# Attention and feed-forward kernel: the product with the values shares three pairs of PSUM banks with the scores and is issued in six pieces

## The chip, the cores and the metric

The kernel runs on one core of a Trainium2 chip. Its engines are PE (TensorE: weight loads and matmuls into PSUM), DVE (VectorE), ACT (ScalarE), POOL (GpSimd) and SP (SyncE, which issues the DMAs). PSUM has eight banks, each of 128 partitions by 512 fp32 numbers. The metric is the device time of one execution in microseconds (us), median of several runs; lower is better.

## What is computed

```
scores = 0.125 * q @ k.T                        # batch 8, heads 8, sequence 576, head width 64
thresh = max(scores, row) - tau
p      = exp(scores - max) where scores >= thresh, else 0
x      = (p / (sum(p, row) + 1e-9)) @ v         # then heads side by side: x is (8, 576, 512)

x_prev = x shifted by one position, zeros first
xk, xr = x_prev + mu_k * (x - x_prev), x_prev + mu_r * (x - x_prev)
out    = sigmoid(xr @ w_r) * (relu(xk @ w_k)**2 @ w_v)     # w_k 512x1024, w_v 1024x512, w_r 512x512
```

## The kernel before

Work comes in 36 **jobs**. A job is one batch and one pair of heads (two of 64 wide, 128 partitions); the first batch's four pairs are each cut in two half jobs, so jobs 1 to 4 hold half the queries and 5 to 8 the other half. A full job has four units `P` of 128 queries for two heads, and one unit `T` for the last 64 queries of both: nine score tiles of 128 x 576. Per tile PE makes the scores (L559, for `T` L526, in the first job L543) as two halves of 288 columns in a pair of PSUM banks, tag `s`; DVE takes the row maximum (L605), ACT the exponential (L621), DVE the mask and the row sum (L629), POOL scales (L654), and DVE transposes in blocks of 32 (L671, for `T` L675). The scores keep the precision of fp32 with q and k each as a high and a low part, which DMAs bring together (`st`, from `hiq`, `loq`, `hik`, `lok`).

When all units of a job are transposed, `attend` multiplies by the values (L705): 144 matmuls of 32 x 64 array tiles, each of which the trace shows as two, so 288 pairs of a weight load and a matmul, into four banks of tag `w`. ACT copies the result to `xT` (L719) and `xE` (L726).

The feed-forward part takes 256 positions of a batch at a time, 18 chunks in all. A chunk has 96 matmuls with `w_k` (L843), 24 with `w_r` (L885) and 48 with `w_v` (L907); each weight and each operand is split in two parts, so a product takes three matmuls. Its PSUM tiles are also of tag `w`. The weights are brought and split in the first part of the run (20 pieces, L355 to L414).

The order on every engine is written by `Plan`. Each step (`add`) has an engine, an assumed time, operands and a key; `order` lists the steps greedily by the earliest start in its own arithmetic, then by the key, to which `NUDGE` adds a number for each kind of step. A buffer is handed out in turn, or to whoever comes first for the tags in `loose`. What the plan lists for an engine is then that engine's instruction order: an engine does not pass a waiting instruction. Two pairs of banks of `s` and four single banks of `w` fill PSUM.

```
ss = {y: psum("s", [P, 2, 512], 2) for y in ys}          # scores
os = [psum("w", [P, 512], 4) for _ in range(4)]          # product with the values
h  = psum("w", [P, 2, CH], 4)                            # feed-forward
KC, MV, RES = 2, 0.031, 3                                # KC: pieces of the product
```

Of the kernel before, what the change touches and what calls it, by code (L numbers as in the profile page):

```python
# [9 lines left out]
AF = mybir.ActivationFunctionType  # L10
# [30 lines left out]
class Step:  # L41
    __slots__ = (
        "eng", "occ", "lat", "fn", "key", "deps", "succ", "allocs", "idx", "missing", "ready",
        "start", "end", "kb", "soft", "att", "kind",
    )


class Plan:

    HOP, LATE, FROM, AHEAD = 0.05, 0.2, 200.0, 1000.0
    SOFT = {"DVE": 0.15, "ACT": 0.15}
    NUDGE = {
# [7 lines left out]
    }  # L62

    def __init__(self):
# [10 lines left out]

    def add(self, eng, occ, fn, reads=(), writes=(), key=0.0, lat=None, kb=0, wait=0.0, kind=None):
        s = Step()
        s.soft = self.SOFT.get(eng, 0.0) if self.soft else 0.0
        s.att = eng == "PE" and key < -500
        if s.att:  # L80
            key += 1000 - self.AHEAD
        s.eng, s.occ, s.fn, s.kb, s.kind = eng, occ, fn, kb, kind
        s.key = key + self.NUDGE.get(kind, 0.0)
# [36 lines left out]
        s.deps.discard(s.idx)  # L120
        self.steps.append(s)
        return s

    def order(self, loose=()):
# [15 lines left out]
        free = {}  # L140
# [4 lines left out]
        for s in steps:  # L145
            if s.missing == 0:
                open_[s.eng].add(s.idx)
        pipe = 0.0
        out = []
        placed = set()  # L150
# [21 lines left out]
        while len(out) < total:  # L172
            best = None
            for e, cand in open_.items():
                f = free[e]
                pick = None
                for i in cand:
                    s = steps[i]
                    t = when(s)
                    if t is None:  # L180
                        continue
                    t = max(t, f)
                    k = (t + s.soft, s.key, i, t)
# [7 lines left out]
            s = steps[i]  # L191
            open_[e].discard(i)
            s.start = t
            free[e] = t + s.occ
            if e == "DMA":
                pipe = max(pipe, t) + s.kb / 260.0
                s.end = max(t + 3.5, pipe + 2.5)
            else:
                s.end = t + s.lat
            for b in s.allocs:  # L200
# [10 lines left out]
            for j in s.succ:  # L211
# [3 lines left out]
                late = self.LATE if n.att and t > self.FROM else 0.0  # L215
                n.ready = max(n.ready, t + s.occ if same else s.end + self.HOP + late)
                if n.missing == 0:
# [12 lines left out]
def tile_threshold_attention_then_rwkv_ffn(  # L230
# [265 lines left out]
    def scores(unit, ss, key):  # L496
# [5 lines left out]
        if unit["kind"] == "T" and not job["plain"]:  # L502
# [17 lines left out]
            for h in range(2):  # L520
                for v_ in range(2):
# [11 lines left out]

                    add("PE", 0.264, mm, reads=[bd, r], writes=[ss[1]], key=key - 1000, lat=0.44, kind="pe1")
            return
        if job["plain"]:
# [13 lines left out]

            add("PE", 3.0, both, reads=[raw], writes=list(ss.values()), key=key - 1000, lat=3.25, kind="pe2")
            return
        for y in range(2):
            st1, st2 = job["st"][y]
            for j, l in enumerate((st1, st2)):
# [10 lines left out]

                add("PE", 0.264, mm, reads=[l, st1], writes=[ss[y]], key=key + 0.5 * y - 1000, lat=0.44, kind="pe3")

    def softmax(unit):
# [6 lines left out]
        sq, c = job["sq"], unit["c"]  # L576
        p = {y: (sq, (c, y)) for y in ys}

# [4 lines left out]

        ss = {y: psum("s", [P, 2, 512], 2) for y in ys}
        scores(unit, ss, float(n))
        for y in ys:
# [95 lines left out]
    def attend(job, key):  # L682
# [9 lines left out]
        tail = [(xE, (b % NE, hp))] if job["tail"] else []  # L692
        os = [psum("w", [P, 512], 4) for _ in range(4)]
        last = job["units"][-1]
        for o in os:
            add("PE", 0.0, lambda: None, reads=[(last["sm"], (RES, 1))], writes=[o, *main, *tail], key=-400.0, lat=0.0, kind="pe4")
        for k in range(KC):

            def mm(k=k):
                for j in range(k * NB // KC, (k + 1) * NB // KC):  # L700
                    for h in range(2):
                        hs = slice(h * D, (h + 1) * D)
                        for a in range(4):
# [8 lines left out]

            occ = (MV * n + 0.3) / KC
            add("PE", occ, mm, reads=[vt, sq], writes=os, key=key - 1000, lat=occ + 0.25, kind="pe5")
        for a in range(4):

            def put(a=a):
                to = x.get()[:, hp, 1 : 1 + SM].rearrange("p (c a i) -> p c a i", a=4, i=Q)
                A.activation(  # L719
                    to[:, cs[0] : cs[-1] + 1, a],  # L720
                    os[a].get()[:, 0 : mid - lo].rearrange("p (c i) -> p c i", i=Q),
                    AF.Copy,
                )

            def put_tail(a=a):
                A.activation(  # L726
                    xE.get()[:, hp, b % NE, 1 + a * QT : 1 + (a + 1) * QT], os[a].get()[:, mid - lo : n], AF.Copy
                )

            add("ACT", 0.16 if len(cs) == 4 else 0.11, put, reads=[os[a]], writes=main, key=key - 5, kind="act8")  # L730
            if job["tail"]:
                add("ACT", 0.07, put_tail, reads=[os[a]], writes=tail, key=key - 5, kind="act9")

# [14 lines left out]
    def ffn_chunk(kind, b0, g, key):  # L748
# [82 lines left out]
        for j in range(NFT // 2):  # L831
            h = psum("w", [P, 2, CH], 4)
            for f in range(2):
                y, o = divmod((2 * j + f) * P, 512)
                fs = slice(o, o + P)
                for ct in range(NCT):
# [10 lines left out]
                    c2 = ct - ct % 2  # L847
                    add("PE", 0.3585, mm, reads=[w, *([xk] if ct == 0 else [(xk, (0, c2)), (xk, (1, c2))])], writes=[h, *([(k2, (0, j))] if f == 0 and ct == 0 else [])], key=key, lat=0.53, kind="pe6")
            js = slice(2 * j, 2 * j + 2)
# [25 lines left out]
        for j in range(CH // P):  # L875
            ts = slice(j * P, (j + 1) * P)
            z = psum("w", [P, DM], 4)
            for ct in range(NCT):
# [8 lines left out]
                c2 = ct - ct % 2  # L887
                add("PE", 0.69, mm, reads=[w, *([xr] if ct == 0 else [(xr, (0, c2)), (xr, (1, c2))])], writes=[z, *([(sg, j)] if ct == 0 else [])], key=key, lat=0.86, kind="pe7")
            add("ACT", 0.49, lambda j=j, z=z: A.activation(sg.get()[:, j], z.get(), AF.Copy), reads=[z], writes=[(sg, j)], key=key - 20, kind="act14")
# [7 lines left out]
        for j in range(CH // P):  # L897
            ts = slice(j * P, (j + 1) * P)
            vps = psum("w", [P, DM], 4)
            for ft in range(NFT):  # L900
# [7 lines left out]

                add("PE", 0.69, mm, reads=[w, *([k2] if ft == 0 else [(k2, (0, ft // 2)), (k2, (1, ft // 2))])], writes=[vps], key=key, lat=0.86, kind="pe8")
            add(  # L910
# [65 lines left out]

    plan.order(loose=("w", "r"))
    plan.issue()
# [41 lines left out]
```

## Time and profile before

| | |
|---|---|
| median of 3 runs | 1134.08 us (1131.31 to 1139.18) |
| the profiled execution | 1133.43 us, of which the span from first to last instruction is 1131.3 us |
| PE busy | 922.5 us, 82% |
| DVE busy | 841.9 us, 74% |
| ACT, POOL busy | 649.1 us, 57%; 573.1 us, 51% |
| mean granted clock of PE | 0.921 of full speed |
| first product, last product | 25.2 us, 993.5 to 1000 us |

The busy time of an engine is the time in which any of its instructions runs by the profile; a matmul's end is modelled, so neighbours overlap. The share of one engine says little here, since the run has stretches of different kinds: the start, in which weights are prepared and the feed-forward work has not begun (to about 113 us), the stretch in which it begins (to about 353 us, the end of the 13th product), a steady stretch of 23 jobs, and after the last product a stretch of feed-forward work alone.

### The profile page before, as it was taken

Reading aid. Unit: us, or ns where it says so; the run is one execution under the profiler, and the core shown is the slowest. Engines: PE = TensorE matmul, PEld = TensorE weight load, DVE = VectorE, ACT = ScalarE, POOL = GpSimd, SP = SyncE. Lnnn points to the kernel's source line nnn. Section 1 sums busy time; section 2 is a strip of 40 time slices with the busy share of each in tenths; the row PEclk is TensorE's granted clock in tenths of the full one; section 3 lists DMA queues with packets and bytes.
Section 4 is the critical chain, followed back from the end, with each engine's and each line's share of the span. In section 5 each row is a group of like instructions: output and inputs, shape, how many; then the busy total and the mean of one; then the engine's idle time right before and its main releaser. Section 6 shows DMA issues by size and latency. Waiting matters only on the chain.

```text
span 1131.3 us, 35156 instructions
## 1 busy us (share of the span) xinstructions
PE 922.5 (82%) x14672; PEld 822.8 (73%) x14672; DVE 841.9 (74%) x1657; ACT 649.1 (57%) x1492; POOL 573.1 (51%) x582
## 2 busy tenths in 40 slices
PE   2334677787688898899899889988989898999988
PEld 2324566776578887888788778877878787888877
DVE  5776977788887888798889798978887988821120
ACT  3434663565456675667576657665766675634432
POOL 3444744454445555565555555555555555443431
PEclk9655788799688999999999999999999999999989
DMA  9376657645444445454545445554545454100000
GB/s 305 110 238 181 213 142 204 175 133 145 128 127 127 141 133 145 129 146 127 139 135 146 127 130 143 131 143 117 146 133 138 128 153 116 57 20 19 20 19 19
DMA packets 57581, 147.83 MB, mean 131 GB/s; under 512 B 9680, under 2 KB 9680, under 8 KB 52816
## 3 DMA queue, kind: packets, MB, share of 16 engines
q1 hardware_dynamic: 57424, 145.60, 45.5%
q8 instruction: 116, 1.90, 0.7%
q14 instruction: 41, 0.34, 0.1%
HBM read 74.19 MB, written 9.44 MB: 74 GB/s over the span
## 4 chain that ended last, share of the span: by engine, by line
PE 49%; DVE 24%; issue 12%; ACT 9%; POOL 5%; DMA 1%; SPq 0%; POOLq 0%; ACTq 0%; DVEq 0%
PE w L705 16%; PE s L559 9%; PE w L843 9%; PE w L907 8%; DVE sq L671 6%; PE w L885 6%; DVE sm L605 6%; DVE sq L629 6%; DVE r L800 3%; ACT sq L621 3%; POOL sq L654 2%; PE s L526 1%; ACT k L856 1%; ACT sm L613 1%; DVE sg L913 1%
## 5 line engine op out<-in xcount | busy, mean ns | idle before, releaser
L654 POOL TENSOR_SCALAR sq<-sq,sm 128x576 f32<-128x576 f32 x288 | 227.3, 802 | 235.5 <-DVE sm L640 228.0
L605 DVE TENSOR_REDUCE sm<-s 128x1 f32<-128x576 f32 x288 | 212.5, 751 | 117.1 <-PE s L559 102.3
L705 PE MATMUL w<-sq,v 32*64 32x144 f32 (+2 forms) x10368 | 193.3, 297 | 121.3 <-issue 98.2
L705 PEld LDWEIGHTS w<-sq,v 32*64 32x64 f32 x10368 | 172.3, 146 | 142.3 <-issue 114.2
L629 DVE SCALAR_TENSOR_TENSOR sq<-s,sm,sq 128x576 f32<-128x576 f32 x288 | 226.2, 803 | 24.7 <-ACT sq L621 23.3
L843 PE MATMUL w<-xk,wk 128*128 128x256 f32 x1728 | 226.9, 289 | 8.1 <-ACT xk L813 4.0
L843 PEld LDWEIGHTS w<-xk,wk 128*128 128x128 f32 x1728 | 221.0, 195 | 11.3 <-POOL xk L821 5.0
L907 PE MATMUL w<-wv,k 128*128 128x512 f32 x864 | 214.8, 396 | 0.4 <-ACT xE L726 0.4
L621 ACT ACTIVATE sq<-s,sm 128x576 f32<-128x576 f32 x288 | 208.9, 726 | 0.2
L671 DVE STREAM_TRANSPOSE sq<-sq 128x1152 f32<-128x1152 f32 x128 | 175.4, 1371 | 16.1 <-POOL sq L654 15.9
L907 PEld LDWEIGHTS w<-wv,k 128*128 128x128 f32 x864 | 161.3, 191 | 31.2 <-ACT xE L726 0.7
L559 PE MATMUL s<-st 128*128 128x288 f32 x504 | 125.4, 333 | 56.9 <-DVE sq L629 41.6
L613 ACT ACTIVATE sm<-sm,small 128x1 f32<-128x1 f32 x288 | 83.8, 291 | 151.1 <-DVE sm L605 139.5
L559 PEld LDWEIGHTS s<-st 128*128 128x128 f32 x504 | 89.5, 205 | 84.0 <-issue 58.8
L821 POOL TENSOR_TENSOR xk<-r,xk 128x512 fp32r<-128x512 f32 x72 | 92.4, 1283 | 101.8 <-ACT xk L813 100.7
L866 POOL TENSOR_TENSOR k<-r,k 128x512 fp32r<-128x512 f32 x72 | 93.9, 1305 | 73.1 <-ACT k L856 73.0
L559 PE MATMUL s<-st,st 128*128 128x288 f32 x504 | 117.0, 315 | 0.6 <-issue 0.6
L800 DVE SCALAR_TENSOR_TENSOR r<-r,mu_sb,xT 128x256 f32<-128x256 f32 x128 | 74.3, 620 | 52.5 <-POOL r L791 44.1
L885 PE MATMUL w<-wr,xk 128*128 128x512 f32 x432 | 107.8, 391 | 0.0
L719 ACT ACTIVATE xT<-w 128x128 f32<-128x128 f32 (+1 forms) x144 | 34.5, 288 | 99.7 <-PE w L705 99.7
L559 PEld LDWEIGHTS s<-st,st 128*128 128x128 f32 x504 | 89.2, 207 | 1.1 <-issue 1.1
L885 PEld LDWEIGHTS w<-wr,xk 128*128 128x128 f32 x432 | 78.1, 188 | 13.2
(55 smaller groups left out, 899.1 us busy)
## 6 DMA issues: line engine op xcount, KB each, us to landing
v<-in_v SPq DMA_DIRECT2D x36, 1152.0 KB, 5.1
st<-hiq SPq DMA_DIRECT2D x140, 144.0 KB, 2.5
st<-loq SPq DMA_DIRECT2D x140, 144.0 KB, 2.6
loq<-in_qk SPq DMA_DIRECT2D x35, 288.0 KB, 2.9
lok<-in_qk SPq DMA_DIRECT2D x35, 288.0 KB, 3.0
st<-hik SPq DMA_DIRECT2D x70, 144.0 KB, 2.8
st<-lok SPq DMA_DIRECT2D x70, 144.0 KB, 3.0
out<-sg SPq DMA_DIRECT2D x32, 256.0 KB, 2.3
```

What stands on the lines that cost most here:

```text
L559: PE.matmul(ss[y].get()[:, z, 0:HS], l.get()[:, c * P : (c + 1) * P], r.get()[:, keys(z)], start=(j == 0), stop=(j == 1),)
L605: lambda sv=sv, col=col: V.tensor_reduce(col(0), sv(), axis=AX.XY, op=ALU.max, negate=True),
L613: lambda col=col: A.activation(col(1), col(0), AF.Identity, bias=small.get()[:, 1:2], scale=-1.0),
L621: lambda st=st, pv=pv, col=col: A.activation(pv(), st(), AF.Exp, bias=col(0)),
L629: lambda st=st, pv=pv, col=col: V.scalar_tensor_tensor(pv(), st(), col(1), pv(), op0=ALU.is_ge, op1=ALU.mult, accum_out=col(2)),
L654: lambda y=y: G.tensor_scalar(part(y), part(y), sm.get()[:, 3, y : y + 1], 0.0, op0=ALU.mult, op1=ALU.add),
L671: V.transpose(t, t)
L705: PE.matmul(os[a].get()[hs, 0:n], vt.get()[rows, j, hs], sq.get()[rows, j, h, lo:hi], start=(j == 0), stop=(j == NB - 1),)
L800: V.scalar_tensor_tensor(d.get()[:, y, o : o + n], diff.get()[:, y, o : o + n], mu_sb.get()[:, j, hc + y : hc + y + 1], prv[:, hc + y], op ...
L843: PE.matmul(h.get()[:, f], l, r, start=(ct == 0 and i == 0), stop=(ct == NCT - 1 and i == 2))
L885: PE.matmul(z.get(), l, r, start=(ct == 0 and i == 0), stop=(ct == NCT - 1 and i == 2))
L907: PE.matmul(vps.get(), l, r, start=(ft == 0 and i == 0), stop=(ft == NFT - 1 and i == 2))
```

## The change

PSUM is divided anew: three pairs of banks with tag `s`, which the scores and the product take from one pool, and two single banks of tag `w` for the feed-forward part alone (`NF = 2`). A product takes two pairs, in which each of its four outputs has a bank of its own as before. It is issued in six pieces of 24 matmuls (48 pairs in the trace) in place of two of 72, and the plan may put other PE work between pieces; a piece carries an earliest start relative to the piece before it (`after`, `GAP`). ACT copies a pair of banks at a time: two `put` and two `put_tail` per job in place of four and four. The plan's arithmetic now counts PE instructions (`ni`) and adds a stall at each 256th by `FETCH`; its soft margins, start times of the weights (`W0` to `W3`) and all key numbers are new (`FIRST` is a second table, for steps with an early key), and `s` and `sm` buffers are no longer handed out in turn.

```diff
-    HOP, LATE, FROM, AHEAD = 0.05, 0.2, 200.0, 1000.0
-    SOFT = {"DVE": 0.15, "ACT": 0.15}
+    HOP, LATE, FROM, AHEAD = 0.05, 0, 200.0, 70.0
+    SOFT = {"DVE": 0.1, "ACT": 0.1}
     NUDGE = {
-        "act1": 6.0, "act10": -16.5, "act11": -27.5, "act12": -14.5, "act13": -6.0, "act14": -29.5, "act15": -3.0,
...
+        "act1": 45.5, "act10": 55.0, "act11": -38.5, "act12": -129.5, "act13": 11.0, "act14": 2.0, "act15": 185.0,
...
+    CHUNK, FETCH = 256, 3.55
...
-                    k = (t + s.soft, s.key, i, t)
+                    late = t + s.soft
+                    if s.after is not None:
+                        late = max(late, s.after[0].start + s.after[1])
+                    k = (late, s.key, i, t)
...
+            stall = 0.0
+            if s.ni:
+                more = self.CHUNK - code % self.CHUNK
+                code += s.ni
+                while more <= s.ni:
+                    at = t + stall + s.occ * more / s.ni
+                    stall += max(0.0, turned + self.FETCH - at)
+                    turned = max(at, turned + self.FETCH)
+                    more += self.CHUNK
+            free[e] = t + s.occ + stall
...
-    W0, W1, W2, W3, AVK = 0.653, 1.950, 42.500, 5.365, 1.0
-    KC, MV, RES = 2, 0.031, 3
+    W0, W1, W2, W3, AVK = 18.804, 1.197, 87.809, 6.640, 1.0
+    KC, MV, RES, NF, SW, GAP = 6, 0.031, 3, 2, 0.2, 0.0135
...
+        ss = {y: psum("s", [P, 2, 512], 3) for y in ys}
+        scores(unit, ss, float(n))
...
-        ss = {y: psum("s", [P, 2, 512], 2) for y in ys}
-        scores(unit, ss, float(n))
...
-        os = [psum("w", [P, 512], 4) for _ in range(4)]
+        os = [psum("s", [P, 2, 512], 3) for _ in range(2)]
...
-                                os[a].get()[hs, 0:n],
+                                os[a // 2].get()[hs, a % 2, 0:n],
...
-        for a in range(4):
+        for a in range(2):
...
             def put(a=a):
-                to = x.get()[:, hp, 1 : 1 + SM].rearrange("p (c a i) -> p c a i", a=4, i=Q)
+                to = x.get()[:, hp, 1 : 1 + SM].rearrange("p (c a i) -> p a c i", a=4, i=Q)
                 A.activation(
-                    to[:, cs[0] : cs[-1] + 1, a],
-                    os[a].get()[:, 0 : mid - lo].rearrange("p (c i) -> p c i", i=Q),
+                    to[:, 2 * a : 2 * a + 2, cs[0] : cs[-1] + 1],
+                    os[a].get()[:, :, 0 : mid - lo].rearrange("p a (c i) -> p a c i", i=Q),
                     AF.Copy,
                 )
...
-            h = psum("w", [P, 2, CH], 4)
+            h = psum("w", [P, 2, CH], NF)
...
-    plan.order(loose=("w", "r"))
+    plan.order(loose=("w", "r", "s", "sm"))
```

What this does to the order is seen at three places. In the rows, names end in a running number of the buffer; `x2` or `x3` is so many equal instructions in a row.

The first place is PE at the start, around the first product (`w_182` to `w_188` before, `s_222` and `s_225` now). Before:

```order
L543 MATMUL s_133<-st_0_70 128x288
L543 MATMUL s_135<-st_0_70 128x288
L705 MATMUL w_182<-sq_120,v_82 64x64
L705 MATMUL w_184<-sq_120,v_82 64x64
...
L705 MATMUL w_186<-sq_120,v_82 64x64
L705 MATMUL w_188<-sq_120,v_82 64x64
L559 MATMUL s_337<-st_1_106 128x288 x2
L559 MATMUL s_337<-st_1_106,st_0_109 128x288 x2
```

Now:

```order
L567 MATMUL s_126<-st_0_78 128x288
L567 MATMUL s_128<-st_0_78 128x288
L583 MATMUL s_139<-st_1_91 128x288 x2
L583 MATMUL s_139<-st_1_91,st_0_94 128x288 x2
L583 MATMUL s_162<-st_2_96 128x288 x2
L583 MATMUL s_162<-st_2_96,st_1_109 128x288 x2
L583 MATMUL s_184<-st_1_91 128x288 x2
L583 MATMUL s_184<-st_1_91,st_0_94 128x288 x2
L729 MATMUL s_222<-sq_119,v_80 64x64 x2
L729 MATMUL s_225<-sq_119,v_80 64x64 x2
```

Three score tiles of the second job now stand ahead of the first job's product; before, all of them stood behind it.

The second place is SP's queue at the start, at the loads for the third job (`loq_258`, `lok_355` before, `loq_136`, `lok_146` now) and the values of the second (`v_344` before, `v_403` now). Before:

```order
L355 DMA wk_0_154<-in_w_k 128x512
L459 DMA loq_258<-in_qk 128x576
L443 DMA v_344<-in_v 128x2304
L459 DMA lok_355<-in_qk 128x576
L490 DMA st_0_409<-hiq_405 64x576
```

Now:

```order
L483 DMA loq_136<-in_qk 128x576
L483 DMA lok_146<-in_qk 128x576
L379 DMA wk_0_150<-in_w_k 128x512
...
L483 DMA loq_397<-in_qk 128x576
L467 DMA v_403<-in_v 128x2304
```

The load of the third job's k has moved ahead of the second job's values.

The third place is PE in the steady stretch, at the product of the 25th job. Before, the product stands in one run (`w_9294` to `w_9300`), with scores and feed-forward matmuls only ahead of it and behind:

```order
L843 MATMUL w_9204<-xk_8901,wk_0_623 128x256 x3
L559 MATMUL s_9282<-st_1_8807 128x288 x2
L559 MATMUL s_9282<-st_1_8807,st_0_8811 128x288 x2
L705 MATMUL w_9294<-sq_8739,v_9007 64x144
L705 MATMUL w_9296<-sq_8739,v_9007 64x144
...
L559 MATMUL s_9456<-st_2_9089 128x288 x2
```

Now (`s_9205`, `s_9208`), with the end of one piece, a feed-forward triple, the next piece, and further on the score tile that stands in this product:

```order
L729 MATMUL s_9208<-sq_8602,v_8921 64x144 x2
L945 MATMUL w_9184<-wv_0_2462,k_0_9006 128x512 x3
L729 MATMUL s_9205<-sq_8602,v_8921 64x144 x2
...
L583 MATMUL s_9333<-st_2_9092 128x288 x2
L583 MATMUL s_9333<-st_2_9092,st_1_9109 128x288 x2
L729 MATMUL s_9205<-sq_8602,v_8921 64x144 x2
```

Between two pieces there are now three feed-forward matmuls or one score tile, where there was nothing.

## Rows read from the trace of the kernel before

**Rows 1.** Windows of four stretches, busy us of each engine.
```profile
core 0: us, PE busy (x) PEld busy (x) DVE busy (x) ACT busy (x) POOL busy (x), PEclk, DMA share, GB/s
0.00:113.00 113.00, 40.88 (x1227) 35.07 (x1228) 79.13 (x138) 44.93 (x97) 49.41 (x46) 0.68 0.70 208
113.00:353.00 240.00, 180.76 (x3302) 161.23 (x3304) 196.65 (x377) 136.01 (x336) 122.65 (x124) 0.83 0.54 153
353.00:1001.00 648.00, 580.40 (x9472) 519.84 (x9454) 545.30 (x1084) 420.92 (x986) 355.51 (x370) 0.99 0.47 131
1001.00:1132.00 131.00, 120.50 (x695) 106.61 (x693) 20.84 (x59) 47.27 (x75) 45.55 (x43) 0.96 0.06 19
```

**Rows 2.** PE, waits between 353 and 1001 us: us, times, longest.
```profile
PE w L705 <- issue: 39.3, 29, 2.0
PE s L559 <- DVE sq L629: 14.9, 13, 2.5
PE w L705 <- DVE sm L639: 6.0, 8, 0.9
```

**Rows 3.** PE, timeline around one product, whole, and part of a second.
```profile
597.54 0.42 PE L559 MATMUL s<-st,st 128*128 128x288 f32 x2
597.89 3.40 PE L705 MATMUL w<-sq,v 32*64 32x144 f32 x194
602.89 1.75 PE L705 MATMUL w<-sq,v 32*64 32x144 f32 x94 [1.61 <-issue]
604.57 0.53 PE L559 MATMUL s<-st 128*128 128x288 f32 x2
604.94 0.43 PE L559 MATMUL s<-st,st 128*128 128x288 f32 x2
605.21 0.43 PE L559 MATMUL s<-st 128*128 128x288 f32 x2
...
629.41 2.27 PE L705 MATMUL w<-sq,v 32*64 32x144 f32 x128 [1.34 <-issue]
632.88 0.50 PE L705 MATMUL w<-sq,v 32*64 32x144 f32 x14 [1.20 <-issue]
```

**Rows 4.** DMA queue of PE's instructions: packets, MB, share.
```profile
q8 instruction: 116, 1.90, 0.7%
```

**Rows 5.** PE, timeline of the feed-forward work after the last product.
```profile
1005.96 11.69 PE L843 MATMUL w<-xk,wk 128*128 128x256 f32 x96
1017.49 5.63 PE L885 MATMUL w<-wr,xk 128*128 128x512 f32 x24
1022.95 11.05 PE L907 MATMUL w<-wv,k 128*128 128x512 f32 x48
1033.84 1.33 PE L843 MATMUL w<-xk,wk 128*128 128x256 f32 x7
```

**Rows 6.** DVE, longest wait, of 0 to 353 us, then of 353 to 1001 us.
```profile
DVE sm L605 <- PE s L559: 39.9, 36, 7.2
...
DVE sm L605 <- PE s L559: 62.5, 77, 4.0
```

**Rows 7.** PE, timeline of the first products.
```profile
46.45 2.59 PE L705 MATMUL w<-sq,v 32*64 32x64 f32 x153 [8.84 <-issue]
62.40 0.82 PE L559 MATMUL s<-st 128*128 128x288 f32 x2 [7.48 <-issue]
```

**Rows 8.** SyncE, timeline: two loads of the second and third head pairs.
```profile
31.89 0.33 SPq L443 DMA_DIRECT2D v<-in_v  x1
32.31 0.38 SPq L459 DMA_DIRECT2D lok<-in_qk  x1
```

**Rows 9.** DVE, timeline: a transpose, then, later, one score tile.
```profile
617.79 1.37 DVE L671 STREAM_TRANSPOSE sq<-sq 128x1152 f32<-128x1152 f32 x1
...
622.11 0.76 DVE L605 TENSOR_REDUCE sm<-s 128x1 f32<-128x576 f32 x1 [0.29 <-PE s L526]
622.96 0.82 DVE L629 SCALAR_TENSOR_TENSOR sq<-s,sm,sq 128x576 f32<-128x576 f32 x1
```

More of the change, by code (lines that the diff above doesn't have):

```diff
@@ L43 @@
         "eng", "occ", "lat", "fn", "key", "deps", "succ", "allocs", "idx", "missing", "ready",
-        "start", "end", "kb", "soft", "att", "kind",
+        "start", "end", "kb", "soft", "att", "kind", "ni", "after",
     )
 class Plan:
-    HOP, LATE, FROM, AHEAD = 0.05, 0.2, 200.0, 1000.0
-    SOFT = {"DVE": 0.15, "ACT": 0.15}
+    HOP, LATE, FROM, AHEAD = 0.05, 0, 200.0, 70.0
+    SOFT = {"DVE": 0.1, "ACT": 0.1}
     NUDGE = {
[7 rows of a table removed]
-    }
[7 rows of a table added]
+    }
+    FIRST, UNTIL = {
[8 rows of a table added]
+    CHUNK, FETCH = 256, 3.55
     def __init__(self):
@@ L74, in buf, with add @@
         return b
-    def add(self, eng, occ, fn, reads=(), writes=(), key=0.0, lat=None, kb=0, wait=0.0, kind=None):
+    def add(self, eng, occ, fn, reads=(), writes=(), key=0.0, lat=None, kb=0, wait=0.0, kind=None, ni=0, after=None):
         s = Step()
@@ L79, in add @@
         s.att = eng == "PE" and key < -500
+        early = (key + 1000 if s.att else key) < self.UNTIL
         if s.att:
             key += 1000 - self.AHEAD
-        s.eng, s.occ, s.fn, s.kb, s.kind = eng, occ, fn, kb, kind
-        s.key = key + self.NUDGE.get(kind, 0.0)
+        s.eng, s.occ, s.fn, s.kb, s.kind, s.ni, s.after = eng, occ, fn, kb, kind, ni, after
+        s.key = key + self.NUDGE.get(kind, 0.0) + (self.FIRST.get(kind, 0.0) if early else 0.0)
         s.lat = occ + 0.1 if lat is None else lat
@@ L148, in order @@
         pipe = 0.0
+        code, turned = 0, -100.0
         out = []
@@ L198, in order @@
             else:
-                s.end = t + s.lat
+                s.end = t + s.lat + stall
             for b in s.allocs:
@@ L215, in order @@
                 late = self.LATE if n.att and t > self.FROM else 0.0
-                n.ready = max(n.ready, t + s.occ if same else s.end + self.HOP + late)
+                n.ready = max(n.ready, t + s.occ + stall if same else s.end + self.HOP + late)
                 if n.missing == 0:
@@ L532, in mm @@
                             )
-                    add("PE", 0.264, mm, reads=[bd, r], writes=[ss[1]], key=key - 1000, lat=0.44, kind="pe1")
+                    add("PE", 0.264, mm, reads=[bd, r], writes=[ss[1], *([unit["p"][1]] if h + v_ == 0 else [])], key=key - 1000, lat=0.44, kind="pe1", ni=4)
             return
@@ L549, in both @@
                         )
-            add("PE", 3.0, both, reads=[raw], writes=list(ss.values()), key=key - 1000, lat=3.25, kind="pe2")
+            add("PE", 3.0, both, reads=[raw], writes=list(ss.values()), key=key - 1000, lat=3.25, kind="pe2", ni=16)
             return
@@ L565, in mm @@
                         )
-                add("PE", 0.264, mm, reads=[l, st1], writes=[ss[y]], key=key + 0.5 * y - 1000, lat=0.44, kind="pe3")
+                add("PE", 0.264, mm, reads=[l, st1], writes=[ss[y], *([unit["p"][y]] if j == 0 else [])], key=key + 0.5 * y - 1000, lat=0.44, kind="pe3", ni=4)
     def softmax(unit):
@@ L576, in softmax @@
         sq, c = job["sq"], unit["c"]
-        p = {y: (sq, (c, y)) for y in ys}
+        p = unit["p"] = {y: (sq, (c, y)) for y in ys}
+        ss = {y: psum("s", [P, 2, 512], 3) for y in ys}
+        scores(unit, ss, float(n))
         def part(y):
@@ L711, in mm @@
                             )
-            occ = (MV * n + 0.3) / KC
-            add("PE", occ, mm, reads=[vt, sq], writes=os, key=key - 1000, lat=occ + 0.25, kind="pe5")
-        for a in range(4):
+            occ = MV * n / KC + SW
+            ni = NB // KC * 32
+            prev = add(
+                "PE",
+                occ,
+                mm,
+                reads=[vt, sq],
+                writes=os,
+                key=key - 1000,
+                lat=occ + 0.25,
+                kind="pe5",
+                ni=ni,
+                after=(prev, GAP * ni) if k else None,
+            )
+        for a in range(2):
             def put(a=a):
-                to = x.get()[:, hp, 1 : 1 + SM].rearrange("p (c a i) -> p c a i", a=4, i=Q)
+                to = x.get()[:, hp, 1 : 1 + SM].rearrange("p (c a i) -> p a c i", a=4, i=Q)
                 A.activation(
-                    to[:, cs[0] : cs[-1] + 1, a],
-                    os[a].get()[:, 0 : mid - lo].rearrange("p (c i) -> p c i", i=Q),
+                    to[:, 2 * a : 2 * a + 2, cs[0] : cs[-1] + 1],
+                    os[a].get()[:, :, 0 : mid - lo].rearrange("p a (c i) -> p a c i", i=Q),
                     AF.Copy,
@@ L726, in put_tail @@
                 A.activation(
-                    xE.get()[:, hp, b % NE, 1 + a * QT : 1 + (a + 1) * QT], os[a].get()[:, mid - lo : n], AF.Copy
+                    xE.get()[:, hp, b % NE, 1 + 2 * a * QT : 1 + 2 * (a + 1) * QT].rearrange("p (a i) -> p a i", a=2),
+                    os[a].get()[:, :, mid - lo : n],
+                    AF.Copy,
                 )
-            add("ACT", 0.16 if len(cs) == 4 else 0.11, put, reads=[os[a]], writes=main, key=key - 5, kind="act8")
+            add("ACT", 0.3 if len(cs) == 4 else 0.2, put, reads=[os[a]], writes=main, key=key - 5, kind="act8")
             if job["tail"]:
-                add("ACT", 0.07, put_tail, reads=[os[a]], writes=tail, key=key - 5, kind="act9")
+                add("ACT", 0.1, put_tail, reads=[os[a]], writes=tail, key=key - 5, kind="act9")
     def edge(b, key):
@@ L847, in ffn_chunk @@
                     c2 = ct - ct % 2
-                    add("PE", 0.3585, mm, reads=[w, *([xk] if ct == 0 else [(xk, (0, c2)), (xk, (1, c2))])], writes=[h, *([(k2, (0, j))] if f == 0 and ct == 0 else [])], key=key, lat=0.53, kind="pe6")
+                    add("PE", 0.3585, mm, reads=[w, *([xk] if ct == 0 else [(xk, (0, c2)), (xk, (1, c2))])], writes=[h, *([(k2, (0, j))] if f == 0 and ct == 0 else [])], key=key, lat=0.53, kind="pe6", ni=6)
             js = slice(2 * j, 2 * j + 2)
```

9 lines of the change are left out of this document (4 added, 5 removed), and 20 rows, old and new, of the table NUDGE.

## The prediction

> **What bounds the kernel now.** I first cut the run into stretches, since the whole-run shares mix different limits [rows 1]. To 353 us PE is busy 40.9 + 180.8 = 222 us and DVE 79.1 + 196.7 = 276 us of 353: neither is full, DVE is nearer. From 353 to 1001 us, the 23 jobs from the 14th to the 36th, PE is busy 580 of 648 us and DVE 545. After 1001 us only feed-forward matmuls are left, PE is busy 120.5 of 131 us and DVE hardly works.
>
> Next I asked what PE waits for in the steady stretch [rows 2]. The largest entry is not an engine: the product at L705 waits 39.3 us in 29 gaps for "issue", nothing that the profile shows. Scores that wait for DVE's mask cost 14.9 us, products that wait for the softmax 6.0 us.
>
> What are these gaps? The timeline of PE shows them inside the product [rows 3]: a run of 128 pairs, an idle 1.20 us, then the rest. The 128 pairs start between 629.41 and 632.88, 3.47 us. A pair is a weight load and a matmul, so 128 pairs are 256 instructions. The DMA queue of instructions moves 116 packets and 1.90 MB [rows 4], 16.4 kB each, and the four stretches list some 14,700 matmuls [rows 1], 127 pairs a packet. So I read the gap as PE waiting for its next 256 instructions: a block may not be shorter than about 3.5 us. The 128 pairs take 2.27 us with the last one's tail, 2.27 - 0.26 = 2.01 us from start to start, 0.0157 us each; all other matmuls are several times longer, so only products meet this limit. The steady stretch's 29 gaps cost 39.3 us and 29 x 0.26 = 7.5 us that the profile counts as busy, 47 us.
>
> The Trainium skill, page "Runtime: NRT & Kernel Launch", section "Instruction fetch mechanics", has the blocks of 256 instructions too, but says that the fetch is hidden because the sequencer dispatches more slowly than the memory fills. The row with 1.20 us idle after just 128 pairs speaks against the second half of this; by it the gaps would have another cause and stay, which is the fourth rival below.
>
> **Stalls removed.** I counted the two orders in blocks of 128 pairs, each matmul at its start-to-start time: 0.0157 us for a product's pair; 0.133 us for a score matmul, from 604.94 to 605.21 for two [rows 3]; 0.120, 0.227 and 0.227 us for the three kinds of feed-forward matmuls, from (1017.49 - 1005.96)/96, (1022.95 - 1017.49)/24 and (1033.84 - 1022.95)/48 [rows 5]. With a block at 3.6 us at least, the order before has 50 short blocks and 73 us of stall; 42 us lie in the second half of the blocks, where the trace shows 47. The new order has 25 short blocks, 14 us, and 4 us in that half. In the steady stretch I take 47 - 4 = 43 us as removed. The rest belongs to the start, below.
>
> **Switches added.** Each time PE goes from full-array matmuls to a product and back, something is lost. Into the product: the last score pair starts at 597.54 and the product at 597.89, 0.35 us in place of 0.27, so 0.08. Out of it: 94 pairs from 602.89 should end at 604.37, the score starts at 604.57, 0.20 later, and its first two matmuls take 0.37 in place of 0.27, 0.10 more [rows 3]. Together 0.38 us. The order had 23 such round trips in the steady stretch and has 127, that is 104 x 0.38 = 40 us added. These rows show scores next to the product; most new neighbours are feed-forward triples, which no row shows in this place. With the entry hidden it is 0.30, with an entry that costs 0.20 more, as much as the exit's first step, 0.58: 31 to 60 us. I keep 40, since a feed-forward matmul has the same full array. So **stalls and switches cancel in the steady stretch**: -43 + 40 = -3 us.
>
> **Work moved.** By my count the order after the last product holds 540 feed-forward matmuls in place of 696: 288 x 0.120 + 252 x 0.227 = 92 us in place of 117, 25 us less. The same 25 us, and some 4 us more, stand in the steady stretch now (571 us of work in place of 543). Up to the 13th product the work is 174 us against 177. PE is the bound of the steady stretch and of the end, so moving costs and gains the same: 0, with 29 - 25 - 4 = 0 when the start is counted.
>
> **Waits in the steady stretch.** DVE waits 62.5 us for scores there, 77 times [rows 6]: before, a product kept PE for some 6.7 us (597.89 to 604.57) and no score could pass. Now a score tile stands inside many products, and outside of them three tiles can be under way in place of two. PE's own waits for DVE, 14.9 + 6.0 = 21 us, should shrink; DVE's 545 us for 23 jobs are 23.7 us a job against PE's 28.2, so DVE has the slack. But while a product runs it holds two of the three pairs, so scores have one pair where they had two. Between all 21 us gone and as much again I take **-10 us**.
>
> **The start, to 353 us.** DVE is the nearer engine, idle 77 us, of which 39.9 us waiting for scores [rows 6]. Two things cause this. The product kept PE, with stalls: the second product starts at 46.45 after 8.84 idle us, and after its end the scores come only at 62.40, 7.48 idle us later [rows 7]. And k of the third job (32.31) is issued right behind values that wait for the first product to end (31.89) on SP's queue [rows 8]. In the new order three score tiles stand ahead of the first product, and the load of k ahead of those values. The 12 pieces of `w_r` and `w_v` are due later, so DVE meets fewer of them in the first jobs; all 20 pieces still come before the 13th product, and feed-forward work by then is equal. The 33 more round trips here (49 in place of 16) are 13 us of PE time that lies beside DVE's, with PE at 222 of 353. Of DVE's 39.9 us I take 30 as saved, with bounds of 0 and 50 us (the waits that remain include ACT, POOL and the first load).
>
> Edits at no cost: ACT copies two banks at a time and is far from full (421 of 648 us [rows 1]); two banks for the feed-forward part suffice while ACT or DVE empties one within the 2.7 us and more that PE takes to fill the other (12 x 0.227).
>
> **Sum.** The profiled execution took 1133.4 us (span 1131.3), 0.7 under the median of 1134.1. 1133.4 - 3 - 10 - 30 = 1090.4, so **1091 us** beside the median.
>
> **Rivals.** (1) Scores flow better than I take it: DVE's wait for scores at the start goes with its followers (50 us) and PE's 21 us of waits go; 1134 - 3 - 21 - 50 = 1060 us. For it: the two largest waits of DVE are of this kind. Against it: one pair for scores while a product runs.
>
> (2) The start doesn't get faster, since DMA, ACT and POOL pace it, and a switch costs 0.46 in place of 0.38, so that switches outweigh stalls by 5 us: 1134 + 5 - 10 = 1129 us, no change. For it: DVE's wait is often only the last of a chain.
>
> (3) One pair is too few: **slower**. A score inside a product waits on PE until DVE has masked the tile before it in that pair, and the rest of the product's pieces are queued behind it. From the start of the maximum (622.11) to the end of the mask (623.78) a tile takes 1.67 us, with its four score matmuls and the hand-over (0.53 and 0.29) 2.5 us; if a transpose of 1.37 us [rows 9] stands between, 3.9 us. Two pieces with what stands between them last about 2 x (0.75 + 0.75) = 3.0 us. So the tile is in time without a transpose and 0.9 us late with one. Two such waits a product are 1.8 x 36 = 65 us: 1091 + 65 = 1156 us. It decides from 43/36 = 1.2 us a product. Against it: the order has one or two tiles inside a product.
>
> (4) The gaps are not the fetch and stay: +43 us in the steady stretch, some 15 at the start: 1150 us. The block count that agrees with the trace (42 against 47 us) speaks against it.
>
> **How the numbers follow.** Forecast 0.50 (about 1075 to 1115), rival 1 0.21, rival 2 0.16, rival 3 0.09, rival 4 0.04. About 1% (11 us) is what a measurement of this kernel can tell from no change. Faster by more: the forecast and rival 1, with a little of rival 2, 0.73; within 1% 0.15; slower 0.12. The range leaves out most of rivals 3 and 4 and the end of rival 1 in which every bound is at its best: **1048 to 1137 us**.
>
> **What would show it.** Right: in the steady stretch L705's wait for "issue" falls from 39 us to under 10; a run of 48 pairs of a product is followed by a feed-forward triple or a score; a round trip costs about 0.4 us; the last product ends near 985 us and the stretch behind it is some 106 us; DVE's wait for scores up to the 13th product falls by half or more, and that product ends near 320 us in place of 353. Wrong: PE idle between pieces with DVE's mask as releaser (rival 3); gaps for "issue" at other places (rival 4); a round trip to the feed-forward of over 0.6 us, which alone would eat the gain.

## The result and the profile after

The changed kernel takes 1082.97 us (median of four runs, 1081.60 to 1085.64) against 1133.56 us on the same chip: ratio 0.9549, 95% interval 0.951 to 0.9589, so 4.5% faster. The forecast was 1091 us in a range of 1048 to 1137. The profiled execution has a span of 1081.8 us (1083.59 us in all) against 1131.3 before.

The boundaries are found from the products at L729, where an end is the start of a product's last matmul: the fourth ends at 97.4 us (110.6 before), the 13th at 323.2 us (353.2), the last at 978.9 us (999.7). The first row of the windows ends with the fourth product; feed-forward work begins at 115.0 us now and began at 112.7. In the windows of the changed kernel PE is now busy 638 of 656 us in the steady stretch:

```profile
core 0: us, PE busy (x) PEld busy (x) DVE busy (x) ACT busy (x) POOL busy (x), PEclk, DMA share, GB/s
0.00:97.00 97.00, 46.17 (x1229) 37.10 (x1230) 70.23 (x131) 42.31 (x88) 45.39 (x44) 0.73 0.73 219
97.00:323.00 226.00, 182.67 (x3269) 153.25 (x3270) 197.33 (x371) 132.20 (x298) 123.68 (x119) 0.83 0.59 173
323.00:979.00 656.00, 637.70 (x9649) 540.22 (x9634) 551.25 (x1104) 423.76 (x913) 372.10 (x385) 0.99 0.47 130
979.00:1082.00 103.00, 94.07 (x551) 83.12 (x540) 17.57 (x52) 36.06 (x59) 34.42 (x34) 0.97 0.07 21
```

PE's waits there, which answer to [rows 2]. The line numbers have moved: L583 scores, L550 scores of the tail unit, L729 product, L881, L923 and L945 feed-forward, L653 DVE's mask:

```profile
PE s L583 <- DVE sq L653: 4.7, 8, 1.2
PE s L583 <- issue: 3.6, 2, 2.0
PE s L583 <- ACT xE L762: 3.3, 5, 1.3
PE w L881 <- ACT r L889: 2.1, 4, 0.7
PE s L729 <- DVE sq L653: 1.8, 4, 0.9
...
PE s L729 <- issue: 0.3, 1, 0.3
```

The product's 39.3 us for "issue" are down to 0.3, and scores wait 4.7 us for the mask in place of 14.9. The timeline of PE in one product (the 25th) answers to [rows 3]:

```profile
661.63 1.04 PE L729 MATMUL s<-sq,v 32*64 32x144 f32 x48
662.60 0.96 PE L945 MATMUL w<-wv,k 128*128 128x512 f32 x3
663.49 1.04 PE L729 MATMUL s<-sq,v 32*64 32x144 f32 x48
664.46 0.97 PE L945 MATMUL w<-wv,k 128*128 128x512 f32 x3
665.36 1.04 PE L729 MATMUL s<-sq,v 32*64 32x144 f32 x48
...
668.20 0.53 PE L583 MATMUL s<-st 128*128 128x288 f32 x2
668.57 0.42 PE L583 MATMUL s<-st,st 128*128 128x288 f32 x2
668.92 1.04 PE L729 MATMUL s<-sq,v 32*64 32x144 f32 x48
```

A piece is 48 pairs with no idle time marked, and something of the full array stands behind each here. In the whole steady stretch the 138 pieces form 127 such runs. The price of that is in the start times: from 661.63 to 663.49 are 1.86 us, of which 48 x 0.0157 = 0.75 for the pairs and 3 x 0.227 = 0.68 for the triple, so 0.43 for the round trip. Around the score tile, the exit from 668.20 to 668.57 is the 0.37 us of [rows 3] again.

DVE's waits, of 0 to 323 us and, below the dots, of 323 to 979 us, answer to [rows 6]:

```profile
DVE sm L629 <- PE s L583: 24.1, 20, 4.7
...
DVE sq L653 <- ACT sm L637: 30.7, 30, 3.6
DVE sm L629 <- PE s L583: 29.9, 24, 6.4
```

DVE's wait for scores fell from 39.9 to 24.1 us at the start and from 62.5 to 29.9 us in the steady stretch, while its wait for ACT (the exponential, or the step ahead of it) has grown in the steady stretch, from 17.3 (`DVE sq L629 <- ACT sq L621: 17.3, 30, 2.5`) to 30.7. The end [rows 5] has 36 matmuls of a chunk left and then three chunks; it lasts 103 us, where it lasted 131:

```profile
978.69 0.47 PE L729 MATMUL s<-sq,v 32*64 32x144 f32 x11
979.09 8.46 PE L945 MATMUL w<-wv,k 128*128 128x512 f32 x36
987.38 11.54 PE L881 MATMUL w<-xk,wk 128*128 128x256 f32 x96
```

For all kernels below I split PE's time by the start times of its matmuls: whatever a start-to-start time has over the nominal one of the prediction is booked as "in the product" (both neighbours are the product's), "round trips" (the steps into the product, out of it, and to the second matmul after it, where the excess is at most 0.35 us), "waits" (every larger excess outside the product, those three steps included) and "small" (the rest). Times in us; "half clock" is the time in the steady stretch that the trace shows at the lower of the two clock levels (1.2 GHz).

| | 13th product ends | steady stretch | work | in the product | round trips (number) | waits | small | half clock |
|---|---|---|---|---|---|---|---|---|
| before | 353.2 | 646.4 | 543.4 | 52.2 | 7.8 (23) | 31.9 | 11.1 | 17 |
| after | 323.2 | 655.6 | 572.2 | 7.3 | 49.2 (127) | 19.6 | 7.5 | 7 |
| two_by_two | 327.7 | 653.4 | 571.8 | 15.6 | 25.9 (67) | 29.0 | 11.1 | 7 |
| three_by_three | 326.4 | 662.9 | 571.7 | 13.5 | 17.6 (46) | 46.5 | 13.8 | 17 |
| run_late | 323.8 | 738.4 | 568.8 | 46.1 | 9.4 (23) | 81.5 | 32.7 | 68 |
| run_all | 365.1 | 744.1 | 570.4 | 49.9 | 9.4 (23) | 84.7 | 29.7 | 58 |
| run_early | 362.8 | 660.7 | 573.8 | 9.9 | 49.4 (127) | 21.6 | 6.0 | 3 |
| old_banks | 329.3 | 669.1 | 529.7 | 39.0 | 29.0 (77) | 61.1 | 10.4 | 41 |
| kc2 | 345.3 | 690.5 | 544.0 | 52.4 | 15.3 (43) | 66.4 | 12.3 | 75 |
| plain_old | 357.1 | 681.0 | 547.4 | 63.0 | 8.5 (23) | 51.9 | 10.1 | 48 |
| plain_new | 338.3 | 725.0 | 561.1 | 23.7 | 43.0 (111) | 78.2 | 19.1 | 92 |

### The profile page after: what moved, and what is told of

Its sections match the earlier page's. It is cut to its first block, busy times and chain, and to the rows that moved or that the text cites. A ratio compares the mean times of both kernels' runs of the same rounds, so it can differ in the third digit from the quotient of the medians.

```text
span 1081.8 us, 34916 instructions
## 1 busy us (share of the span) xinstructions
PE 960.6 (89%) x14672; PEld 813.7 (75%) x14672; DVE 836.4 (77%) x1657; ACT 634.3 (59%) x1358; POOL 575.6 (53%) x582
## 4 chain that ended last, share of the span: by engine, by line
PE 60%; DVE 26%; ACT 5%; issue 5%; POOL 2%; DMA 0%; SPq 0%; ACTq 0%; POOLq 0%
PE w L881 15%; PE s L729 14%; PE w L945 11%; PE s L583 10%; PE w L923 8%; DVE sq L653 7%; DVE sm L629 6%; DVE sq L695 4%; DVE r L838 3%; PE s L550 2%; DVE sm L663 1%; ACT sq L645 1%; POOL sq L678 1%; DVE sm L664 1%; DVE sg L951 1%
## 5 line engine op out<-in xcount | busy, mean ns | idle before, releaser
L629 DVE TENSOR_REDUCE sm<-s 128x1 f32<-128x576 f32 x288 | 208.2, 746 | 70.2 <-PE s L583 54.0
L653 DVE SCALAR_TENSOR_TENSOR sq<-s,sm,sq 128x576 f32<-128x576 f32 x288 | 225.9, 801 | 38.7 <-ACT sm L637 38.3
L729 PE MATMUL s<-sq,v 32*64 32x144 f32 (+2 forms) x10368 | 220.9, 297 | 32.5 <-issue 15.3
L881 PE MATMUL w<-xk,wk 128*128 128x256 f32 x1728 | 235.3, 289 | 6.4 <-ACT xk L851 2.3
L881 PEld LDWEIGHTS w<-xk,wk 128*128 128x128 f32 x1728 | 220.2, 195 | 17.1 <-issue 7.1
L729 PEld LDWEIGHTS s<-sq,v 32*64 32x64 f32 x10368 | 171.6, 144 | 77.6 <-issue 65.9
L945 PE MATMUL w<-wv,k 128*128 128x512 f32 x864 | 220.4, 399 | 2.1 <-ACT sg L927 1.5
L945 PEld LDWEIGHTS w<-wv,k 128*128 128x128 f32 x864 | 157.5, 189 | 41.5 <-issue 8.7
L583 PE MATMUL s<-st 128*128 128x288 f32 x504 | 126.2, 334 | 62.7 <-DVE sq L653 33.5
L583 PEld LDWEIGHTS s<-st 128*128 128x128 f32 x504 | 86.2, 202 | 92.2 <-issue 64.5
L583 PE MATMUL s<-st,st 128*128 128x288 f32 x504 | 115.6, 313 | 0.0
L923 PE MATMUL w<-wr,xk 128*128 128x512 f32 x432 | 108.8, 393 | 0.2 <-POOL wr L438 0.2
L838 DVE SCALAR_TENSOR_TENSOR r<-r,mu_sb,xT 128x256 f32<-128x256 f32 x128 | 76.5, 637 | 35.2 <-POOL r L829 16.2
L851 ACT ACTIVATE xk<-r 128x512 fp32r<-128x512 f32 x72 | 45.2, 627 | 93.9 <-DVE r L838 93.8
L923 PEld LDWEIGHTS w<-wr,xk 128*128 128x128 f32 x432 | 77.8, 188 | 14.7 <-POOL wr L438 0.6
L583 PEld LDWEIGHTS s<-st,st 128*128 128x128 f32 x504 | 87.5, 204 | 1.0 <-issue 0.8
L637 ACT ACTIVATE sm<-sm,small 128x1 f32<-128x1 f32 x288 | 77.8, 288 | 0.0
```

The source lines that it names most:

```text
L583: PE.matmul(ss[y].get()[:, z, 0:HS], l.get()[:, c * P : (c + 1) * P], r.get()[:, keys(z)], start=(j == 0), stop=(j == 1),)
L629: lambda sv=sv, col=col: V.tensor_reduce(col(0), sv(), axis=AX.XY, op=ALU.max, negate=True),
L653: lambda st=st, pv=pv, col=col: V.scalar_tensor_tensor(pv(), st(), col(1), pv(), op0=ALU.is_ge, op1=ALU.mult, accum_out=col(2)),
L729: PE.matmul(os[a // 2].get()[hs, a % 2, 0:n], vt.get()[rows, j, hs], sq.get()[rows, j, h, lo:hi], start=(j == 0), stop=(j == NB - 1),)
L838: V.scalar_tensor_tensor(d.get()[:, y, o : o + n], diff.get()[:, y, o : o + n], mu_sb.get()[:, j, hc + y : hc + y + 1], prv[:, hc + y], op ...
L881: PE.matmul(h.get()[:, f], l, r, start=(ct == 0 and i == 0), stop=(ct == NCT - 1 and i == 2))
```

## The experiments

**Pieces put together again, order otherwise kept.** Five kernels take the changed kernel's finished order and only move pieces up behind an earlier piece of the same product, in all jobs or a part. What stood between them then stands behind; banks, loads and the other engines' orders are the same, so they stay those that were fitted to open products.

```diff
+    plan.gather(6, 1, 36)    # run_all; run_late 6, 14, 36; run_early 6, 1, 13; two_by_two 2, 1, 36; three_by_three 3, 1, 36
     plan.issue()
...
+    def gather(self, size, first, last):     # self.products: a list of a product's six steps for each job
+        order, done, runs = [], set(), {}
+        for j, g in enumerate(self.products):
+            if first <= j + 1 <= last:
+                for p in range(0, len(g), size):
+                    runs[g[p]] = g[p : p + size]
+        for i in self.out:
+            if i not in done:
+                for x in runs.get(i, [i]):
+                    order.append(x)
+                    done.add(x)
+        self.out = order
```

> The changed kernel, with pieces 2 to 6 of every product moved up right behind piece 1 on PE; nothing else in the order changes. Round trips in the steady stretch 127 to 23 (about -42 us at 0.4 us), short blocks of 256 instructions bring back some 43 us of stall there and 22 us up to the 13th product. My theory (stalls and switches cancel in the steady stretch, the gain is the start and the waits): steady stretch equal but for some 10 us of waits, start 10 us longer, together about 1103 us. Rival, that cutting the product in pieces is the gain: back to 1120 us or more. Rival, that only the new banks and the order at the start count: 1083 us.

Measured: 1218.24 us, ratio 1.0685 to the kernel before (1.0648 to 1.0722), which took 1139.7 us on that chip. Not near the 1103 us of my theory; slower than before the change. The 13th product ends 42 us later than in the changed kernel and the steady stretch is 88 us longer; the two runs below take these two parts one at a time.

> As the run before, but only the products of jobs 14 to 36 are put together. My theory: the first 13 jobs as in the changed kernel (to 323 us), the steady stretch within 0 and 12 us of its 656 us, together 1083 to 1095 us. If the pieces were the gain: 35 us or more is lost here.

Measured: 1170.35 us, ratio 1.0262 (1.0225 to 1.0298). The start is that of the changed kernel (323.8 us), and the steady stretch takes 738.4 us, 83 more. The timeline shows a product whole again, with the gap:

```profile
670.93 4.20 PE L747 MATMUL s<-sq,v 32*64 32x144 f32 x255 [0.88 <-DVE sq L670]
676.05 0.74 PE L747 MATMUL s<-sq,v 32*64 32x144 f32 x29 [0.92 <-issue]
```

and these are PE's waits in the steady stretch, with scores at L600 and L567 and the product at L747:

```profile
PE s L600 <- DVE sq L670: 35.9, 21, 3.3
PE s L747 <- issue: 33.3, 28, 2.2
PE s L600 <- ACT xE L781: 15.7, 9, 2.8
PE s L567 <- DVE sq L670: 11.3, 7, 2.6
PE s L600 <- issue: 3.5, 3, 1.6
```

By the table, 39 us come back inside the products (46.1 for 7.3) and 40 go with the round trips (9.4 for 49.2): **these two cancel, as forecast**. What I had not seen is the rest: waits grow by 62 us and "small" by 25. The waits are those of scores for a pair: 35.9 + 11.3 us for DVE's mask and 15.7 us for ACT's copy of the product, against 4.7 and 3.3 in the changed kernel. And with them the granted clock falls, in the window of this stretch:

```profile
324.00:1062.00 738.00, 629.38 (x9604) 558.13 (x9602) 549.26 (x1102) 418.89 (x908) 368.19 (x383) 0.95 0.42 116
```

0.95 for 0.99, 68 us at half clock for 7, which is where matmuls get longer without a gap: 25 of the 33 us of "small" lie in these 68 us. Each fall comes in or behind idle time of PE: PE idles 2.6 us from 385.1 us on and the clock falls at 387.3, it idles 2.2 us from 784.7 on and the clock falls at 786.7.

> Only the products of jobs 1 to 13 are put together (round trips 49 to 13, stall by the block count 10 to 32 us). My theory: the 13th product ends 5 to 15 us later, the rest is equal: 1088 to 1098 us. If PE's blocking at the start had been what cost the 30 us, some 25 us are lost: 1108 us; if only the order of loads and scores had, nothing: 1083 us.

Measured: 1128.76 us, ratio 0.9903 (0.987 to 0.9936). The 13th product ends at 362.8 us, 40 later than in the changed kernel, where I expected 5 to 15 and the first rival 25. Where it is lost says more than the sum. The fifth product ends at 148.0 us before the change, at 117.4 after it and at 128.3 here. So 11 of the 40 us are lost by then and 29 in jobs 6 to 13; and of the 31 us that the change had gained by the fifth product, 20 are still there with the products closed.

> The pieces are put together two by two, so a product is three runs of 96 pairs with the same other work between. Round trips in the steady stretch 127 to 67 (60 x 0.4 = -24 us), stall by the block count 5.0 to 7.3 us; up to the 13th product 49 to 33 and 9.9 to 15.6 us. My theory, that PE bounds the steady stretch and a round trip costs it 0.4 us: -20 us, 1063 us. Rival, that waits for scores take what PE saves: 1083 us.

Measured: 1086.63 us, ratio 0.9529 (0.9505 to 0.9553), against 0.9549 of the changed kernel, the same. The price of a round trip holds: 60 fewer, 49.2 - 25.9 = 23.3 us less, 0.39 each. But waits and "small" grew by 13 us and the products' own gaps by 8, and the steady stretch is 2 us shorter in place of 22. The total is the rival's. PE's first waits there:

```profile
PE s L600 <- ACT xE L781: 7.8, 8, 2.4
PE s L600 <- DVE sq L670: 6.7, 10, 1.1
PE s L747 <- issue: 6.0, 9, 1.4
```

> The changed order, with the pieces put together three by three: two runs of 144 pairs with the same work between and behind. Round trips in the steady stretch 127 to 46 (-31 us), stall by the block count 5 to 18 us. With waits that grow between those of two_by_two (15 us more than in the changed kernel) and of run_late (90 us more): some 45 us more, so 1083 - 31 + 13 + 45 = 1110 us. If PE's own account decided: 1065 us.

Measured: 1096.45 us, ratio 0.9627 (0.9581 to 0.9674). The waits, 46.5 us, are 27 more than in the changed kernel; the expectation had 45. So with the order held, runs of one, two, three and six pieces stand at 0.955, 0.953, 0.963 and 1.068 of the kernel before: the fewer the openings, the more scores wait, and from runs of three on the saved round trips no longer pay for it.

**Is the gap the instruction fetch?**

```diff
+                            if wide == 2:                       # jobs 14 to 36 of run_late
+                                rhs = rhs.unsqueeze(1).broadcast_to([Q, 2, n])
-                                os[a // 2].get()[hs, a % 2, 0:n],
+                                os[a // 2].get()[hs, a % 2, 0 : wide * n],
```

> As run_late (products of jobs 14 to 36 in one run each), but each matmul of those products streams its columns twice, the second time into unused columns of the same bank. Same number of instructions, about 0.031 us a pair in place of 0.0157, so 128 pairs last some 4.0 us, longer than the 3.5 us of a block. If the gaps are PE's instruction fetch, PE's waits of the product for issue in the steady stretch go from 33 us to under 5, though the product itself is longer (9 us). If the gaps belong to the product or its banks, idle times of 1.2 us stay at every 128 pairs.

Measured: the 288 pairs of a product take 8.99 us without a break (a single execution, 1226.45 us in all):

```profile
737.74 2.88 PE L968 MATMUL w<-wv,k 128*128 128x512 f32 x12
740.55 8.99 PE L751 MATMUL s<-sq,v 32*64 32x288 f32 x288
```

PE's longest waits in the steady stretch, 329 to 1118 us, no longer have the product (L751) for "issue" among them; in run_late it was the second with 33.3 us:

```profile
PE s L600 <- DVE sq L670: 37.9, 23, 3.3
PE s L600 <- ACT xE L785: 16.2, 8, 2.8
PE s L567 <- DVE sq L670: 11.3, 7, 2.6
PE s L600 <- issue: 3.4, 3, 1.6
```

The same instructions, banks and neighbours, but 128 pairs now last 128/288 of it, 4.0 us, and the gap is gone. It belongs to a count of instructions in too short a time. The traces also hold the transfers of PE's instruction queue (q8 of [rows 4]), 16,384 bytes each. In the steady stretch of the kernel before, 31 steps inside products have a start-to-start time of over 0.3 us, and 30 of them end 2.2 to 3.1 us after such a transfer began. In wide_late four such steps are left, and none ends so.

The Trainium skill, page "Runtime: NRT & Kernel Launch", section "Instruction fetch mechanics", says that the fetch is hidden because instructions are dispatched more slowly than blocks are filled. The traces do not agree for pairs of 0.0157 us.

**Banks, pieces and plan made anew.** Here the plan makes another order, with the same tables of key numbers.

```diff
-        ss = {y: psum("s", [P, 2, 512], 3) for y in ys}        # old_banks (NF = 4, copies as before)
+        ss = {y: psum("s", [P, 2, 512], 2) for y in ys}
-        os = [psum("s", [P, 2, 512], 3) for _ in range(2)]
+        os = [psum("w", [P, 512], 4) for _ in range(4)]
-    KC, MV, RES, NF, SW, GAP = 6, 0.031, 3, 2, 0.2, 0.0135     # kc2
+    KC, MV, RES, NF, SW, GAP = 2, 0.031, 3, 2, 0.2, 0.0135
-    W0, W1, W2, W3, AVK = 18.804, 1.197, 87.809, 6.640, 1.0    # weights_early; old_weights_late the other way round
+    W0, W1, W2, W3, AVK = 0.653, 1.950, 42.500, 5.365, 1.0
```

> The changed plan with all its tables and six pieces, but PSUM as before: two pairs for scores, four banks shared by the product and the feed-forward part, four copies by ACT. The plan then puts 77 round trips into the steady stretch in place of 127 (-20 us) and 20 us of stall by the block count in place of 5 (+15 us): PE's account is even. Theory that the new banks matter, since the feed-forward part has no bank while a product runs and only scores can stand between pieces: more waits, 1095 to 1120 us. Rival, that pieces alone are the change: 1080 us.

Measured: 1154.64 us, ratio 1.0141 (1.0092 to 1.0191), above the range of my theory.

> The changed kernel with two pieces of 72 matmuls (as before the change) and the plan knowing it. Round trips in the steady stretch 43 in place of 127 (-33 us), stall by the block count 28 in place of 5 us (+23 us). If only the PE account counted: 1075 us. Theory after run_late, that a long run of the product keeps scores from the one pair that they have: waits of 30 us and more on top, and some 10 us at the start, 1100 to 1125 us.

Measured: 1169.07 us, ratio 1.0273 (1.0213 to 1.0333), above the range of my theory.

> The changed kernel with the start times of the 20 weight pieces as before the change. The plan reshuffles (round trips in the steady stretch 103, stall 17 us: -9 + 12 us). If the later weights are part of what made the start shorter, the 13th product ends 5 to 15 us later than 323 us and the total is about 1095 us; if not, 1083 us.

Measured: 1172.20 us, ratio 1.0284 (1.0222 to 1.0347), for a change of four start times, where I expected some 1095. None of the three is faster than the kernel before, and weights_early, which leaves banks and pieces alone, loses as much as kc2. So the three don't tell what a bank or a piece is worth: they also leave the order to which the tables were fitted. That asked for a pair without tables.

```diff
-    NUDGE = { ... }     # plain_old, and with FIRST plain_new
+    NUDGE = {}
```

> The changed kernel with both tables of key numbers empty, so that banks, pieces and the plan's count of PE instructions remain, without numbers fitted to this order. After old_banks, kc2 and weights_early, all of which let the plan make another order than the one the numbers were fitted to and came out at 1155 to 1172 us, I expect 1150 to 1190 us. If banks and pieces bring the gain by themselves: under 1110 us.

Measured: 1184.73 us, ratio 1.0401 (1.0359 to 1.0443).

> The kernel before with its table of key numbers empty. If the numbers are worth as much here as in the changed kernel and the structure is worth the rest of the 51 us, this takes 50 us or so longer than plain_new, 1200 to 1240 us. If the gain of the change is the fitted order alone, it takes the same as plain_new.

Measured: 1171.11 us, ratio 1.0288 (1.0233 to 1.0343). **Without the tables of key numbers the kernel with the new banks and pieces is 1% slower than the old**, not faster: neither of my two expectations. It is one order of each, and both keep other numbers of their own, such as the start times of the weights; four of these alone moved the changed kernel by 8%. So a difference of 1% between two orders does not weigh the structures. The steady stretch in the windows of plain_new:

```profile
338.00:1063.00 725.00, 650.92 (x9581) 554.64 (x9567) 537.42 (x1093) 418.89 (x902) 364.35 (x379) 0.94 0.43 118
```

and of plain_old:

```profile
357.00:1038.00 681.00, 597.84 (x9474) 535.38 (x9477) 554.79 (x1093) 419.10 (x983) 360.27 (x374) 0.96 0.46 125
```

The stall inside products is smaller by 39 us and the start by 19, as in the fitted pair, but 34 us of round trips come with it, and waits (78 for 52 us) and the clock (0.94 for 0.96) go the wrong way.

> The kernel before with the weights' start times of the changed kernel, the counterpart of weights_early (which cost the changed kernel 8%). If any order that the numbers were not fitted to costs this much: 1180 to 1220 us. If the old structure bears it, 1130 to 1150 us. If later weights are a gain by themselves, under 1125 us.

Measured: 1217.81 us, ratio 1.0684 (1.0638 to 1.073). The kernel before bears a foreign set of start times no better (7% lost, against 8%).

## Why the prediction was right

**The gap and its cost.** Right. 47 us were to shrink by 43; the table, which counts every excess inside products, has 52.2 and 7.3, 45 less, and wide_late and the transfers of the instruction queue show the cause. The fourth rival fell with it.

**Round trips.** Right: 0.38 us each, 40 us added; measured (12.0 into the product, 23.8 out of it and 13.4 behind) 49.2 us for 127, 0.39 each, 41 us more than before. Feed-forward neighbours cost about what scores do (0.43 at 661.63). That stalls and switches cancel is shown twice, by before against after and by run_late against after.

**Work moved.** Right: 29 us more work in the steady stretch and 28.7 us less at the end, where I had 25 (1131.3 - 999.7 = 131.6 us before, 1081.8 - 978.9 = 102.9 now).

**Waits in the steady stretch.** The size was right, 10 us forecast and 12.3 measured (31.9 to 19.6), with 4 us more in "small". The reason given was too small a part: I set the pieces' value against the stall alone. run_late shows that this order on the new banks can't do without them: one pair for scores and a whole product in its way cost 62 us of waits and 25 us of "small", with 61 us more at half clock. The third rival named this place (one pair too few) for scores inside an open product; there it didn't happen, and scores behind a closed one wait for a pair in this way. No run changes the banks alone with the order held, so what three pairs give by themselves is not shown.

**The start.** The total is right, the way to it only in part. The stretch was to end near 320 us (30 us of waits saved and 4 us less work); it ends at 323.2, 30.0 us earlier than before. But the 30 us were to come out of DVE's 39.9 us of waiting for scores, and these fell by 16 us. DVE's busy time fell from 276 to 268 us, and the remaining 6 us lie in its other waits. So the term was mis-sized at its source, and that the total fits is in part luck. The open product is not the whole cause either: run_early keeps 20 of the 31 us that are gained by the fifth product, with all these products closed. Closed products do cost this order 40 us up to the 13th. What the earlier load of k, the score tiles ahead of the first product and the later weights give was not tried apart; weights_early doesn't tell, since its order differs everywhere.

**The sum.** 43 us forecast, 50.6 measured in the medians and 49.5 in the spans. By stretches, my terms give -34 for the start, 29 - 3 - 10 = 16 for the steady stretch and -25 for the end; measured are -30.0, 9.2 and -28.7.

**What the prediction didn't say.** I read round trips, blocks and neighbours from the order itself, and much of the gain hangs on that order. With both tables empty, plain_new against plain_old, 1184.73 against 1171.11 us, layout and pieces gave nothing in the one pair of orders that was tried. In shares of the kernel before, the tables are worth 0.0288 to the old kernel, 33 us, and 1.0401 - 0.9549 = 0.0852 to the new one, 97 us. How much of the 51 us the structure would bring in orders fitted equally well is not shown. Why the foreign orders lose this much is open: the rows show more waits and 40 to 90 us at half clock in the steady stretch, and no run separates the one from the other.

## What to carry to other kernels

Count a kernel's PE instructions in blocks of 256 and compare each block's time with the 3.5 us seen here: where a long run of tiny matmuls stays under it, PE idles for its instructions, and cutting the run gains that idle time less what the switches to other work cost (here 0.39 us each, and the two cancelled). Look for the larger effect in who gets through the opening; here it was the score tiles, and the same order with products open or closed took 0.955 or 1.068 of the old time. And when a change comes with a newly fitted order, try both structures without the fit, in several orders each, before crediting the structure.

## What the runs showed of the hardware

- A block of 256 PE instructions took some 3.2 to 3.5 us at the least: 3.47 in [rows 3], and the shortest distance between two starts on the instruction queue is 3.24 us (plain_old). With the columns doubled, 4.0 us a block, the gap was gone (wide_late).
- Going from full-array matmuls to 32 x 64 tiles and back costs 0.38 to 0.41 us in four kernels (49.2/127, 25.9/67, 17.6/46, 9.4/23), and part of it, 0.1 us (13.4/127), shows only at the second matmul after the product. In the other orders of the table, where more of these steps count as waits, it is 0.34 to 0.41.
- A lower granted clock goes with waits: run_late had 62 us more waits in the steady stretch than the changed kernel, and 68 us at 1.2 GHz in place of 7. That the waits bring the falls about is argued from the idle time ahead of them, and no run sets the two apart.
